# LSH attention with two gated MoE layers on one core: head 0's hash bits in a pair of score banks, a later identity load, and idle matmuls in the first gap

## The chip, the cores and the metric

One core of one Trainium2 chip runs the whole program in one launch. The metric is device time in microseconds (us), the median of several executions. A profiled execution has its own time beside it, and a span from its first to its last instruction.

## The reference, cut to what matters

```python
q_bits = (einsum('bhsd,dk->bhsk', q, proj) > 0)      # 6 bits for each of 768 positions, 16 heads of 64
k_bits = (einsum('bhsd,dk->bhsk', k, proj) > 0)
mask = bucket(q_bits)[..., :, None] == bucket(k_bits)[..., None, :]
scores = where(mask, scale * q @ k.T, -1e9)
attn = softmax(scores)                               # then attn @ v
x = attn_out as (1536, 512)
h = x @ w_in;  g = max(h, 0) + alpha * min(h, 0);  y = g @ w_out
h2 = y @ w_in2;  g2 = P(h2) / (Q(h2) + 1e-6);      out = g2 @ w_out2    # P cubic, Q = 1 + |b0||h2| + |b1|h2^2
```

All data are float32. The second half has d_model 512 and d_ff 2048.

## The kernel before, in words

**Work per head.** q and k come in transposed, 64 rows of 768 columns, held twice over 128 partitions. `k2` and `qh` are rounded copies of k and q, `kx` is what is left of k (and minus k on the lower rows), `ql` what is left of q. A row block of 128 queries makes a score tile 128x768 in two PSUM banks, in two steps: `first` (qh against kx, two matmuls of 384 columns, L559) and `second` (ql against k2, two matmuls, L564). The hash bits stand in rows 64 to 75 of `ql` and of `k2`, so `second` needs them: equal bits leave a score alone, unequal bits push it far away. VectorE then clamps the score (L574), ScalarE takes the exponential with the row sum (L580), TensorE turns the block by six transposes against the identity `idf` (L606, called `flip`), ScalarE or VectorE takes it out of PSUM into `pt` (`take`), and after six blocks twelve matmuls multiply with v (`pv`, L649).

**Hash bits.** `bits_mm` (L480) multiplies q and k with the projection: four matmuls of 384 columns, two for q and two for k, into four strips of 32 partitions of one PSUM bank (tag `b`). For head 0 four VectorE operations `bits_at` (L489), each 12 partitions by 384 columns, compare with a threshold and write the bits right into `ql` and `k2`. Later heads use one operation on all strips (L485) and small DMAs (L496). Blocks 0 to 2 of head 0 need only three of the four `bits_at`, since their queries lie in the first half of q.

**The start.** The engines begin with a memset of `rt`, nine matmuls of zeros on it (`warm`, L833, results never read), the constants from ScalarE's DMA queue, and then on SyncE's queue in this order: the identity, k and q of head 0, two weight pieces, q and k for later heads, v. The score tiles rotate through three pairs of banks (tag `s`), which scores and flips share, in the order in which the program text creates them.

**Order of the work.** Nothing is ordered by hand. The code creates tasks with their buffers; a planner (`Plan.order`) gives each task a start time from assumed durations, and the instructions of all engines are emitted by these times. At each step it takes, among the tasks that can begin about first, the one with the highest rank plus bias:

```python
t = max((t for t in ready if t.at[1] <= low), key=lambda t: t.rank + t.bias)
```

The rank is the length of the chain behind the task. The bias, and factors that make the planner prefer one engine to another for a task that may run on several, stand in the table `FAVOUR` by kind of task. A dependency of data is `after`, one of order alone `follow`. Once emitted, each engine runs its instructions in that order. Outside the attention the same planner orders the weight conversions (VectorE and ScalarE split each weight into a high and a low part), the first layer's and the second layer's matmuls (L679, L695, L698: 512 columns each), and the activations.

Of the kernel before, what the change touches and what calls it, by code (L numbers as in the profile page):

```python
# [64 lines left out]
FAVOUR = {
    "a_abs": (62.5, {}), "a_abs2": (202.2, {}), "a_exp": (-128.3, {"act": 0.17}), "a_g": (215.5, {}),
    "a_log": (1470.9, {"act": 0.52}), "a_mul": (-173.3, {"dve": 0.41, "pool": 0.47}), "a_n1": (584.8, {"dvp": 0.91}),
    "a_n2": (0, {"dvp": 0.84}), "a_p0": (-441.7, {"act": 3.65}), "a_p1": (240.4, {"act": 4.27}),
    "a_prep": (-94.8, {}), "a_quad": (-13, {"dvp": 0.98}), "a_sq": (89.8, {"act": 2.63}),
    "a_sum": (284.5, {"dve": 8.45, "pool": 0.09}), "awayb": (10.5, {}), "back": (-63.1, {"act": 0.05, "dvp": 0.04}),  # L70
    "backb": (672.3, {"act": 0.11, "dvp": 17.38}), "banks": (604.6, {"none": 1.11}), "bits": (205.6, {"pe": 2.45}),
    "bits0": (392.1, {"pe": 1.69}), "bits_at0": (-21.4, {}), "bits_at1": (-74.2, {}), "bits_at2": (-64.8, {}),
    "bits_at3": (-18.9, {}), "bits_ev": (-82.2, {"dvp": 0.3}), "bits_evb": (-222.6, {"dvp": 2.87}),
    "bits_mv": (310.2, {"dma": 2.11}), "bits_mvb": (5.8, {"dma": 0.57}), "bitsb": (-952.5, {"pe": 0.94}),
    "c_abs": (-16, {"act": 0.63}), "c_bits": (1.7, {"dve": 5.95}),
    "c_hi": (103.9, {"act": 0.14, "dve": 2.31, "pool": 23.21}), "c_lo": (1216.6, {"dve": 0.24}),
    "c_load": (18.4, {"dma": 0.12, "none": 3.41}), "c_prep": (-597.3, {"dve": 0.7}), "c_tail": (0, {"act": 0.38}),
    "clamp": (-286.8, {"dvp": 2.08}), "clampb": (35.5, {"dvp": 8.19}), "e_abs": (206.6, {"act": 2.31}),
    "e_bits": (-1934.6, {"dve": 0.36}), "e_lo": (-449.7, {"dve": 1.15}), "e_load": (147.1, {"dma": 0.27}),
    "e_out": (492.7, {}), "e_tail": (-99.1, {"act": 0.42}), "expo": (0, {"act": 0.67}),  # L80
    "expob": (-266, {"act": 1.51}), "eye": (239.2, {"dma": 2.17}), "f_abs": (-100.4, {"act": 1.32}),
    "f_bits": (-6, {}), "f_lo": (101.1, {"dve": 1.31}), "f_load": (819.2, {}), "f_out": (18.8, {}),
    "f_tail": (-511.9, {"act": 1.09}), "first": (239.8, {}), "flip": (4, {}), "flipb": (194, {"pe": 0.78}),
    "g_both": (-4.2, {}), "g_both0": (-3, {"dvp": 0.77}), "g_both1": (0, {"dvp": 0.39}),
    "g_hi": (-560.6, {"act": 0.68, "dvp": 47.43}), "g_hi0": (259, {"act": 5.33, "dvp": 1.56}),
    "g_hi1": (-238, {"act": 0.02, "dvp": 0.87}), "g_hi2": (-458.1, {"act": 0.14, "dvp": 0.3}), "g_lo": (142, {}),
    "g_lo0": (-144.9, {"dvp": 0.28}), "g_lo1": (2, {"dvp": 1.07}), "g_lo2": (251.9, {"dvp": 0.85}),
    "g_neg": (587.5, {"act": 1.54}), "g_neg0": (159.4, {"act": 6.17}), "g_neg1": (-0.9, {"act": 7.94}),
    "guard": (-19.6, {}), "guardb": (-1503.1, {"dve": 1.6}), "k2": (-9.1, {"act": 4.28, "dve": 50.0, "pool": 2.03}),
    "k20": (-339.4, {"act": 0.24, "dve": 32.94, "pool": 50.0}),  # L90
    "k2b": (28.3, {"act": 0.26, "dve": 1.26, "pool": 0.08}), "kx": (18.4, {"dve": 2.0}), "kx0": (0.7, {}),
    "kxb": (-433.4, {"dve": 8.17}), "load": (14.8, {"dma": 8.2}), "load0": (1.8, {}), "load2": (-302.2, {}),
    "load2b": (-81.7, {}), "loadb": (-131.6, {"dma": 2.11}), "o_add1": (-4732, {"dvp": 2.93}), "o_add2": (5.8, {}),
    "o_ev": (717.8, {"act": 1.21, "dvp": 0.02}), "o_ev0": (-19.1, {"act": 2.26, "dvp": 18.44}),
    "o_ev2": (632.5, {"act": 18.15, "dvp": 0.03}), "over": (-468.4, {"dvp": 0.04}), "overb": (271.3, {"dvp": 0.48}),
    "pv": (-688, {"pe": 1.11}), "pvb": (40.1, {}), "qh": (-33.7, {"act": 0.02, "dve": 0.44, "pool": 9.08}),
    "qh0": (-225.7, {"act": 1.4, "dve": 50.0, "pool": 0.11}),
    "qhb": (395.9, {"act": 0.03, "dve": 10.86, "pool": 0.02}), "ql": (366.3, {"dve": 7.18, "pool": 0.32}),
    "ql0": (106, {"dve": 8.57, "pool": 0.12}), "qlb": (12.8, {"dve": 10.81, "pool": 7.82}),
    "recip": (-2.7, {"dve": 2.0}), "recipb": (-158.2, {"dve": 0.51}), "reload": (-163.2, {"dma": 0.45}),  # L100
    "s1": (-17, {"pe": 0.73}), "s10": (-1021.8, {}), "s11": (-871.8, {"pe": 1.31}), "s12": (12.5, {}),
    "s2": (-121.5, {"pe": 5.53}), "s20": (0, {"pe": 2.84}), "s21": (-42.4, {"pe": 0.75}),
    "scores": (-47.9, {"pe": 2.11}), "scores0": (-8.7, {}), "scoresb": (53.1, {}), "second": (-269.4, {}),
    "swap": (-61.6, {}), "take": (7.1, {"act": 0.02, "dvp": 50.0}), "takeb": (0, {"act": 0.02, "dvp": 0.11}),
# [936 lines left out]
```

## Time and profile before

| what | value |
|---|---|
| median of 3 runs | 757.69 us (756.81 to 758.21) |
| profiled execution, its own time | 757.42 us |
| its span | 755.6 us |
| PE (TensorE) busy in the span | 744.4 us, 99% |
| mean granted TensorE clock | 0.997 of full |

The first two rows are device times, of unprofiled runs and of the execution that left the profile. The span leaves out what lies before the first and behind the last instruction. PE is TensorE's matmuls, PEld its weight loads, DVE VectorE, ACT ScalarE, POOL GpSimd, SP SyncE; SPq marks DMA issues on SP's queue.

### The profile page before, as it was taken

The page shows a single profiled execution, that of the slowest core. Times are in us where ns is not written, and L with a number is a line of the kernel's source. Part 1 is how long each engine was busy: PE and PEld are TensorE (multiplying, and loading weights), DVE is VectorE, ACT ScalarE, POOL GpSimd, SP SyncE. Part 2 cuts the span into 40 slices and gives each one's busy share as a digit, 9 for nine tenths or more (in the row PEclk, how much of TensorE's full clock was granted, in tenths as well). Part 3 has the DMA queues.
Part 4 walks back from the last instruction along what each step waited for, and adds up shares of the span by engine and source line. Part 5 has one row for each costly group of instructions (what it writes and reads, how often), then busy time and mean ns, then how long its engine had stood idle before and what let it go on. Part 6 is the DMA issues. An engine that isn't in the chain of part 4 may idle for free.

```text
span 755.6 us, 10816 instructions
## 1 busy us (share of the span) xinstructions
PE 744.4 (99%) x3729; PEld 587.2 (78%) x3729; DVE 664.4 (88%) x1187; ACT 513.3 (68%) x881; POOL 146.2 (19%) x130
## 2 busy tenths in 40 slices
PE   7999999999999999999999999999999999999998
PEld 4677667676777888888888888888888888888886
DVE  6998999999989999998999899999898877778882
ACT  5889989978874654544454356887887686766660
POOL 4322211010000000000000000125533344433430
PEclk9999999999999999999999999999999999999999
DMA  6854666556332123256433652520202200200012
GB/s 231 238 172 132 184 181 162 175 189 190 121 109 67 72 96 112 100 179 194 139 108 117 208 173 93 195 112 1 111 1 112 111 1 1 111 1 1 14 57 97
DMA packets 36199, 88.21 MB, mean 117 GB/s; under 512 B 8800, under 2 KB 11952, under 8 KB 34608
## 3 DMA queue, kind: packets, MB, share of 16 engines
q1 hardware_dynamic: 35856, 87.35, 35.7%
q8 instruction: 29, 0.48, 0.2%
q14 instruction: 26, 0.21, 0.1%
q10 hardware_dynamic: 288, 0.17, 0.1%
HBM read 70.62 MB, written 15.78 MB: 114 GB/s over the span
## 4 chain that ended last, share of the span: by engine, by line
PE 93%; DMA 4%; DVE 2%; issue 1%; SPq 0%; POOL 0%; ACT 0%; DVEq 0%; ACTq 0%; POOLq 0%
PE h L679 35%; PE o L698 17%; PE o L695 16%; PE pv L649 8%; PE t L606 7%; PE s L559 4%; PE s L564 4%; DMA rq<-qT 2%; PE h L695 1%; DMA rq<-qN 1%; PE pb L480 1%; DVE x L574 1%; DVE acc L655 0%; DMA k<-bt 0%; DVE kx L466 0%
## 5 line engine op out<-in xcount | busy, mean ns | idle before, releaser
L679 PE MATMUL h<-xh,wih 128*128 128x512 f32 x384 | 150.2, 391 | 0.0
L679 PE MATMUL h<-xl,wih 128*128 128x512 f32 x384 | 149.8, 390 | 0.0
L679 PE MATMUL h<-xh,wil 128*128 128x512 f32 x384 | 149.4, 389 | 0.0
L574 DVE TENSOR_SCALAR_CACHE_REDUCE x<-s 128x768 f32<-128x768 f32 x96 | 90.8, 953 | 7.3 <-PE s L564 6.2
L580 ACT ACTIVATE x<-x,st 128x768 f32<-128x768 f32 x96 | 89.3, 931 | 8.3 <-DVE x L574 4.9
L606 PEld LDWEIGHTS t<-idf,x 128*128 128x128 f32 x576 | 65.8, 141 | 24.3 <-issue 8.5
L429 ACT ACTIVATE pt<-t 128x768 f32<-128x768 f32 x91 | 73.0, 806 | 16.8 <-PE t L606 16.5
L679 PEld LDWEIGHTS h<-xl,wih 128*128 128x128 f32 x384 | 72.1, 188 | 15.5
L679 PEld LDWEIGHTS h<-xh,wil 128*128 128x128 f32 x384 | 72.1, 188 | 15.2
L679 PEld LDWEIGHTS h<-xh,wih 128*128 128x128 f32 x384 | 72.1, 188 | 14.9
L606 PE MATMUL t<-idf,x 128*128 128x128 f32 x576 | 80.7, 277 | 2.8 <-ACT x L580 1.9
L744 POOL TENSOR_TENSOR x<-x,ap 128x512 f32<-128x512 f32 x48 | 62.5, 1303 | 100.6 <-ACT x L732 63.9
L698 PE MATMUL o<-woh,gl 128*128 128x512 f32 x192 | 74.9, 390 | 0.0
L698 PE MATMUL o<-woh,gh 128*128 128x512 f32 x192 | 74.8, 390 | 0.0
L698 PE MATMUL o<-wol,gh 128*128 128x512 f32 x192 | 74.8, 390 | 0.0
L649 PE MATMUL pv<-pt,vr 128*64 128x384 f32 x384 | 68.8, 494 | 0.0
L695 PE MATMUL o<-gh,wol 128*128 128x512 f32 x176 | 68.6, 390 | 0.0
L695 PE MATMUL o<-gh,woh 128*128 128x512 f32 x176 | 68.6, 390 | 0.0
L695 PE MATMUL o<-gl,woh 128*128 128x512 f32 x176 | 68.5, 389 | 0.0
L438 DVE TENSOR_TENSOR gl<-h,gh 128x512 fp32r<-128x512 f32 x96 | 64.8, 684 | 2.3 <-ACT gh L429 1.6
L429 ACT ACTIVATE gh<-h 128x512 fp32r<-128x512 f32 x72 | 43.0, 601 | 28.6 <-DVE h L718 16.9
L329 ACT ACTIVATE raw<-raw 128x512 uint32<-128x512 uint32 x64 | 43.0, 672 | 25.9 <-DMA raw<-w_out 12.9
(97 smaller groups left out, 1449.3 us busy)
## 6 DMA issues: line engine op xcount, KB each, us to landing
raw<-w_in SPq DMA_DIRECT2D x32, 512.0 KB
raw<-w_out SPq DMA_DIRECT2D x32, 512.0 KB
rk<-kT SPq DMA_DIRECT2D x16, 384.0 KB
rq<-qT SPq DMA_DIRECT2D x16, 384.0 KB
sp<-mag SPq DMA_DIRECT2D x24, 256.0 KB
sp<-w SPq DMA_DIRECT2D x16, 256.0 KB
vr<-vN SPq DMA_DIRECT2D x8, 384.0 KB
rs<-rd SPq DMA_DIRECT2D x32, 96.0 KB
```

The costliest lines, as they stand in the source:

```text
L329: s_.activation(self.low, self.low, AF.Copy, scale=2.0 ** -9 * (1 - 2.0 ** -22))
L429: s_.activation(out, in_, AF.Copy, scale=scale)
L438: eng[e].tensor_tensor(out, a, b, op=ALU.subtract)
L559: te.matmul(sp[:, j, :HALF], K["qh"][:, q], K["kx"][:, j * HALF:(j + 1) * HALF], start=True, stop=False)
L574: v_.tensor_scalar(x.rearrange("p (j c) -> p j c", j=2), T["s"][:, :, :HALF], SCALE, FAR, op0=ALU.mult, op1=ALU.min, accum_out=T["st"])
L580: s_.activation(T["x"], T["x"], AF.Exp, bias=T["st"], scale=-1.0, accum_out=tr["ss"][:, half, tt:tt + 1])
L606: te.transpose(o[:, c], T["x"][:, c], idf)
L649: te.matmul(T["pv"][64 * half:64 * half + 64, :HALF], tv["vr"][:, m, kt, :], E[half][0]["pt"][:, kt, :], start=(kt == 0), stop=(kt == NT - 1))
L679: te.matmul(hp, wt[:, kc, f], xt[:, kc], start=(n == 0), stop=(n == 3 * KC - 1))
L695: te.matmul(op, lt[:, m, d], rt, start=(n == 0), stop=(n == 3 * FT - 1))
L698: te.matmul(op, lt[:, d], rt[:, m], start=(n == 0), stop=(n == 3 * FT - 1))
L744: eng[e].tensor_tensor(P[a], P[a], P[b], op=op)
```

## The change

- **Bits of head 0.** Four matmuls as before, but into a pair of banks of tag `s`: q in partitions 0 to 31, k in 64 to 95, the two halves of the columns in the two banks. Two `bits_at` of 12 partitions by 768 columns write them down, one for `ql`, one for `k2`. All blocks of head 0 need both. The pair takes the first slot of the rotation, so the blocks' slots move on by one (`WIDE` by one more).
- **Identity.** Its load follows the load of head 0's q on SP's queue instead of standing ahead of it.
- **Matmuls without use.** Eight more matmuls of zeros (`again`), after `second` of block 2 of head 0, into the bank that `warm` used.
- **Text order.** In head 0 three blocks, not two, are created before the first flip, which changes the order in which scores and flips take slots.
- **Planner.** The assumed wire time of head 0's q goes from 1.0 to 1.6, and nearly all entries of `FAVOUR` (bias and engine factors) are new. So the emitted order of the whole program can differ.

```diff
+AGAIN = 8
 FAVOUR = {
...
-    "eye": (239.2, {"dma": 2.17}),
+    "eye": (-66.1, {"dma": 2.17}),
...
-    "qh0": (-225.7, {"act": 1.4, "dve": 50.0, "pool": 0.11}),
+    "qh0": (656.5, {"act": 0.19, "dve": 2.91, "pool": 0.02}),
...
-    "take": (7.1, {"act": 0.02, "dvp": 50.0}), "takeb": (0, {"act": 0.02, "dvp": 0.11}),
+    "take": (339, {"act": 0.02, "dvp": 5.94}), "takeb": (103.5, {"act": 0.03, "dvp": 0.73}),
...
-WIDE = (3, 2 * NT * HW)
+WIDE = (3, 2 * NT * HW + 1)
...
+        def bits0_mm(e):
+
+            T["b"] = bank_pair("pb0")
+            for j in range(2):
+                for n, r in enumerate(("rq", "rk")):
+                    te.matmul(T["b"][64 * n:64 * n + 32, j, :HALF], Z[n], T[r][:, j * HALF:(j + 1) * HALF],
+                              start=True, stop=True)
+
...
         def bits_at(n):
-            to, j, r = T["ql" if n < 2 else "k2"], n % 2, slice(32 * n, 32 * n + 2 * NB)
-            v_.tensor_scalar(to[64:64 + 2 * NB, j * HALF:(j + 1) * HALF], P["b"][r, :HALF],
-                             cst[r, 0:1], cst[r, 1:2], op0=ALU.is_ge, op1=ALU.mult)
+            r = slice(64 * n, 64 * n + 2 * NB)
+            v_.tensor_scalar(T["k2" if n else "ql"][64:64 + 2 * NB].rearrange("p (j c) -> p j c", j=2),
+                             T["b"][r, :, :HALF], cst[r, 0:1], cst[r, 1:2], op0=ALU.is_ge, op1=ALU.mult)
...
-            plan.send("load" + z, load(n, src), 0.4, 1.0, (), [r])
+            plan.send("load" + z, load(n, src), 0.4, 1.6 if h == 0 and n == "rq" else 1.0, (), [r])
...
-        if h < 2 or h % 2 == 0:
+        if h == 0:
+            b = plan.buf("s")
+            plan.add("bits0", bits0_mm, {"pe": 0.98}, [*R, BZ], [b], cols=1536)
+        elif h == 1 or h % 2 == 0:
...
-            B["at"] = [Buf() for n in range(4)]
-            for n in range(4):
-                plan.add(f"bits_at{n}", lambda e, n=n: bits_at(n), {"dvp": 0.7}, [b, *([B["kx"]] * (n > 1))], [B["at"][n]])
+            B["at"] = [Buf() for n in range(2)]
+            for n in range(2):
+                plan.add(f"bits_at{n}", lambda e, n=n: bits_at(n), {"dvp": 0.88}, [b, *([B["kx"]] * n)], [B["at"][n]])
...
-            at = [BK["at"][half], *BK["at"][2:]]
+            at = BK["at"]
...
-                plan.add("second", second, {"pe": 0.35}, [BK["ql"], BK["k2"], *at], [B["s"]], cols=614)
+                u = plan.add("second", second, {"pe": 0.35}, [BK["ql"], BK["k2"], *at], [B["s"]], cols=614)
+                if t == 2:
+                    w = plan.add("again", again, {"pe": 0.2267 * AGAIN}, [BR], [BPV], cols=512 * AGAIN)
+                    w.after([u])
...
+    PV = {}
+
     def warm(e, count=WARMUP):
 
-        o = tl(ps, "pv", [128, 512], F32, "warm")
+        if not PV:
+            PV["o"] = tl(ps, "pv", [128, 512], F32, "warm")
         for n in range(count):
-            te.matmul(o, rt[:, :128], rt, start=True, stop=True)
+            te.matmul(PV["o"], rt[:, :128], rt, start=True, stop=True)
+
+    def again(e):
+        warm(e, AGAIN)
...
-    plan.send("eye", eye_load, 0.42, 0.25, (), [BE])
+    EYE = plan.send("eye", eye_load, 0.42, 0.25, (), [BE])
...
+    EYE.follow(plan.tags["raw_qk"][1].writers[0])
...
-            wait(2)
+            wait(3 if h == 0 and t < NT - 1 else 2)
```

## Rows read from the trace of the kernel before

**Rows 1.** The page's busy table: engine, busy us, share of the span, instructions.

```profile
PE 744.4 (99%) x3729; PEld 587.2 (78%) x3729; DVE 664.4 (88%) x1187; ACT 513.3 (68%) x881; POOL 146.2 (19%) x130
```

**Rows 2.** Busy time by stretch: length, engines, granted clock, DMA share, GB/s.

```profile
1.40:6.10 4.70, 4.22 (x11) 2.85 (x12) 1.27 (x5) 2.09 (x3) 1.17 (x4) 1.00 0.87 258
6.10:12.90 6.80, 3.92 (x21) 2.35 (x21) 5.38 (x11) 3.02 (x6) 2.66 (x2) 1.00 0.98 373
12.90:17.30 4.40, 4.28 (x24) 2.88 (x24) 3.71 (x7) 3.56 (x7) 1.62 (x3) 0.61 0.32 124
17.30:31.30 14.00, 12.69 (x87) 8.24 (x83) 12.96 (x27) 12.13 (x22) 5.82 (x4) 1.00 0.68 195
31.30:200.00 168.70, 167.28 (x1113) 119.95 (x1110) 157.81 (x315) 147.60 (x258) 28.76 (x31) 1.00 0.59 174
200.00:750.00 550.00, 550.00 (x2479) 449.55 (x2478) 482.02 (x826) 344.66 (x589) 105.39 (x82) 1.00 0.27 93
750.00:755.60 5.60, 2.04 (x9) 1.34 (x8) 0.80 (x3) 0.00 (x0) 0.00 (x0) 0.91 0.27 94
```

**Rows 3.** The same view in stretches of 1 us around the lower clock.

```profile
13.00:14.00 1.00, 1.00 (x9) 1.00 (x9) 0.96 (x4) 1.00 (x3) 0.00 (x0) 0.93 0.98 384
15.00:16.00 1.00, 1.00 (x6) 0.67 (x4) 0.80 (x2) 0.33 (x1) 0.70 (x1) 0.50 0.06 22
17.00:18.00 1.00, 1.00 (x11) 0.52 (x4) 0.89 (x2) 1.00 (x4) 0.90 (x1) 0.86 0.00 0
```

**Rows 4.** The chain of waits, first 40 us: start, length, what.

```profile
8.89 7.26 DMA rq<-qT
16.19 1.42 PE pb L480 x8
...
22.18 0.43 PE s L564
...
23.11 7.35 DMA rq<-qN
...
30.50 0.85 PE pb L480 x8
```

**Rows 5.** Timeline of PE: start, length, instruction [idle before <- releaser].

```profile
1.45 4.21 PE L833 MATMUL warm<-rt 128*128 128x512 f32 x9 [1.45 <-DVE rt L858]
6.09 0.85 PE L480 MATMUL pb<-rq,zq 128*32 128x384 f32 x2 [0.43 <-DMA rq<-qT]
...
6.70 0.68 PE L480 MATMUL pb<-rq,zq 128*32 128x384 f32 x2
6.83 0.61 PE L480 MATMUL pb<-rk,zk 128*32 128x384 f32 x2
7.37 1.31 PE L559 MATMUL s<-kx,qh 128*128 128x384 f32 x6
9.69 1.28 PE L564 MATMUL s<-k,ql 128*128 128x384 f32 x6 [1.00 <-DVE k L489]
12.85 0.88 PE L606 MATMUL t<-idf,x 128*128 128x128 f32 x6 [1.88 <-ACT x L580]
```

**Rows 6.** Timeline of SP's queue.

```profile
0.73 0.38 SPq L844 DMA_DIRECT2D idf<-eye  x1
1.17 0.42 SPq L462 DMA_DIRECT2D rk<-kT  x1
```

**Rows 7.** Timeline of DVE and ACT.

```profile
7.48 0.69 DVE L489 TENSOR_SCALAR k<-pb,every 12x384 fp32r<-12x384 f32 x1 [1.27 <-PE pb L480]
...
9.57 0.67 DVE L489 TENSOR_SCALAR ql<-pb,every 12x384 fp32r<-12x384 f32 x1
...
10.30 0.43 DVE L338 TENSOR_SCALAR mag<-mag 128x512 f32<-128x512 f32 x1
...
10.76 0.96 DVE L574 TENSOR_SCALAR_CACHE_REDUCE x<-s 128x768 f32<-128x768 f32 x1
...
14.54 0.79 ACT L429 ACTIVATE pt<-t 128x768 f32<-128x768 f32 x1
```

More of the change, by code (lines that the diff above doesn't have):

```diff
@@ L71 @@
[L71 to L92, printed above, removed]
@@ L108 @@
[L108 to L112 removed]
+    "a_abs": (-88.3, {}), "a_abs2": (324.8, {}), "a_exp": (-201.2, {"act": 0.17}), "a_g": (-11.7, {}),
@@ new lines @@
+    "a_log": (17.3, {"act": 0.52}), "a_mul": (-448.2, {"dve": 1.24, "pool": 0.62}), "a_n1": (36, {"dvp": 0.91}),
+    "a_n2": (-41.5, {"dvp": 0.84}), "a_p0": (-236.2, {"act": 3.65}), "a_p1": (377.6, {"act": 4.27}),
+    "a_quad": (14.4, {"dvp": 0.98}), "a_sq": (11.1, {"act": 2.63}), "a_sum": (538.1, {"dve": 21.94, "pool": 0.07}),
+    "again": (227.4, {}), "away": (-138.6, {}), "awayb": (-8.9, {}), "back": (0, {"act": 0.05, "dvp": 0.04}),
+    "backb": (35.4, {"act": 0.11, "dvp": 17.38}), "banks": (-122.1, {"none": 1.11}), "bits": (155.7, {"pe": 2.45}),
@@ new lines @@
+    "bits0": (-354.9, {"pe": 1.69}), "bits_at0": (-496.3, {}), "bits_at1": (-811.2, {}),
+    "bits_ev": (-107.6, {"dvp": 0.3}), "bits_evb": (773.6, {"dvp": 2.87}), "bits_mv": (0, {"dma": 2.11}),
+    "bits_mvb": (-334.3, {"dma": 0.57}), "bitsb": (-905.6, {"pe": 0.94}), "c_abs": (0, {"act": 0.63}),
+    "c_bits": (-34.6, {"dve": 5.95}), "c_hi": (3.7, {"act": 0.16, "dve": 0.93, "pool": 20.78}),
+    "c_lo": (521.7, {"dve": 0.24}), "c_load": (18.8, {"dma": 0.12, "none": 3.41}), "c_prep": (-463.8, {"dve": 0.7}),
@@ new lines @@
+    "c_tail": (-41.9, {"act": 0.38}), "clamp": (-81.4, {"dvp": 2.08}), "clampb": (-7.4, {"dvp": 8.19}),
+    "e_abs": (-132.7, {"act": 2.31}), "e_bits": (-3077, {"dve": 0.36}), "e_lo": (-153.9, {"dve": 1.15}),
+    "e_load": (-541.4, {"dma": 0.27}), "e_out": (476, {}), "e_tail": (-523.3, {"act": 0.42}),
+    "expo": (41.7, {"act": 0.67}), "expob": (26.7, {"act": 1.51}), "eye": (-66.1, {"dma": 2.17}),
+    "f_abs": (-279.1, {"act": 1.32}), "f_bits": (-23.9, {}), "f_lo": (1247.2, {"dve": 1.31}), "f_load": (535.9, {}),
@@ new lines @@
+    "f_out": (25.1, {}), "f_tail": (-1291.2, {"act": 1.09}), "first": (79, {}), "flip": (-181.6, {}),
+    "flipb": (387.4, {"pe": 0.78}), "g_both": (55.8, {}), "g_both0": (73.1, {"dvp": 0.77}),
+    "g_both1": (-394, {"dvp": 0.39}), "g_hi": (-929.9, {"act": 0.1, "dvp": 18.51}),
+    "g_hi0": (182.2, {"act": 8.91, "dvp": 0.03}), "g_hi1": (-172.7, {"act": 0.02, "dvp": 0.46}),
+    "g_hi2": (-568.9, {"act": 0.17, "dvp": 1.07}), "g_lo": (-385.1, {}), "g_lo0": (-7.9, {"dvp": 0.28}),
+    "g_lo1": (1.6, {"dvp": 1.07}), "g_lo2": (160.8, {"dvp": 0.85}), "g_neg": (-21.4, {"act": 1.54}),
@@ new lines @@
+    "ql0": (-135.5, {"dve": 0.13, "pool": 0.03}), "qlb": (0, {"dve": 50.0, "pool": 49.26}),
+    "recip": (-182.1, {"dve": 2.0}), "recipb": (-620.4, {"dve": 0.51}), "reload": (486.4, {"dma": 0.45}),
+    "s1": (-133.5, {"pe": 0.73}), "s10": (185.5, {}), "s11": (0, {"pe": 1.31}), "s12": (3.2, {}),
+    "s2": (20.2, {"pe": 5.53}), "s20": (7.2, {"pe": 2.84}), "s21": (13.9, {"pe": 0.75}),
+    "scores": (41.4, {"pe": 2.11}), "scores0": (7.4, {}), "scoresb": (269.4, {}), "second": (-808.9, {}),
+    "swap": (177.6, {}), "take": (339, {"act": 0.02, "dvp": 5.94}), "takeb": (103.5, {"act": 0.03, "dvp": 0.73}),
@@ L161, in send @@
         t.wire, t.begin, t.ack, t.block = wire, begin, ack, block
+        return t
     @staticmethod
@@ L858, in lsh_attention_moe_moe @@
     plan.add("zero", lambda e: v_.memset(rt.bitcast(F32), 0.0), {"dve": 1.0}, writes=[BR])
-    plan.add("warm", warm, {"pe": 0.2267 * WARMUP}, [BR], [plan.buf("pv")], cols=512 * WARMUP)
+    BPV = plan.buf("pv")
+    plan.add("warm", warm, {"pe": 0.2267 * WARMUP}, [BR], [BPV], cols=512 * WARMUP)
     plan.add("c_load", consts_load, {"none": 3.1}, writes=[BZ])
     plan.add("c_prep", consts_prep, {"dve": 0.3}, [BZ], [BZ])
-    plan.send("eye", eye_load, 0.42, 0.25, (), [BE])
+    EYE = plan.send("eye", eye_load, 0.42, 0.25, (), [BE])
     plan.add("a_prep", last_prep, {"dve": 0.1}, [BZ], [BL])
```

42 lines of the change are left out of this document (18 added, 24 removed).

## The prediction

> **What bounds the kernel now.** First the busy table [rows 1]: TensorE is busy 744.4 of 755.6 us, idle 11.2. Then the windows [rows 2], to see where those 11.2 lie. Take the length of each stretch less PE's busy time: 1.40 before the first row, 0.48 to 6.1 us, 2.88 to 12.9, 0.12 to 17.3, 1.31 to 31.3, 1.42 from there to 200, nothing from 200 to 750, 3.56 in the last stretch (last evictions and stores). So 95% of the span is a full PE queue, and no edit at the front changes it except by bringing it forward. What can be won at the front is idle PE time between 1.4 and 31.3 us, 4.79 us, and time at the lower clock.
>
> For that, the clock column: 0.61 in the stretch 12.9 to 17.3 [rows 2]. The 1 us windows show the edges [rows 3]: 0.93, then 0.50, then 0.86, so from about 13.86 to 17.28 the lower level of 1.2 GHz is granted, 3.4 us. PE had been idle 1.88 us just before, from 10.97 to 12.85, and 1.00 us ahead of 9.69 [rows 5]. PE was busy in nearly all of the slow stretch, so about 3.3 x 0.5 = 1.65 us of it were lost.
>
> Next, what released the work at the front: the PE timeline [rows 5] and the chain of waits [rows 4]. The bits wait for head 0's q (6.09), `second` for VectorE's bits (9.69), the first flip for the exponential (12.85); later the chain is head 1's q, issued at 8.89 and landed at 16.15, its bits, and through small DMAs its `second` at 22.18; then the bits of a later pair, whose q lands at 30.46. Behind that PE waits almost never.
>
> **The change, part by part.** Times are on the profiled execution's axis.
>
> *Identity later.* Its issue takes SP from 0.73 until 1.17 [rows 6]; without it everything behind goes 0.44 us earlier. It also carried 64 KB, 0.25 us at 258 GB/s [rows 2], so head 0's q lands 0 (if the queue's rate alone sets it) to 0.69 us earlier; I take 0.44, the issue. It is used up to the point where `warm` holds PE: nine matmuls from 1.45 end at 5.66 [rows 5], against a start of the bits at 6.09. So the bits start near 5.65, 0.44 earlier. The identity itself is next late: one 64 KB transfer behind q, needed by the first flip at 12.85. Those 6 us are its cover; without them each 0.1 us of delay would reach the flip.
>
> *Bits in a pair of banks.* Before, the four matmuls sit in four different strips and run side by side: two sets of records, 0.61 us apart at the lower clock (6.09 and 6.70), done at 7.44 [rows 5]; at full clock all eight take 0.85 [rows 4]. Now q's two halves use the same strip, and k's two also, so the second half follows the first: four sets instead of two. At the lower clock that is 4 x 0.61 + 0.13 = 2.6 us, at full clock twice 0.85 less one drain, about 1.5. The level rose during the old bits (first record 0.85, last 0.61), near 7.0. From 5.65 to 7.0 some 2.2 sets pass, the other 1.8 take 0.3 each and a drain of 0.2: done at 7.75, against 7.44. Bounds: 7.15 (full clock throughout) and 8.25 (low throughout).
>
> *Two evictions instead of four.* They go at 0.695 us each (7.48 to 9.57 for three steps [rows 7]), but `second` waited only for three: 2.21 us from 7.48 to 9.69. The 12x768 form isn't in the trace. Below, the clamp of 128x768 follows its like by 0.88 and lasts 0.96 [rows 7]; above, two old ones, 1.39. I take 1.0, nearest to the clamp, which reads as many PSUM columns. So two take 2.0, and `second` starts near 7.8 + 2.0 + 0.15 = 9.95 instead of 9.69 (9.1 to 11.3). The edit removes an operation off the path and none on it.
>
> *Slots.* Block 2's `first` now needs the bank pair that the bits hold, so it can't run in the gap ahead of `second`; one pair, a third of the 1.05 us by which three are streamed (1.31 with the drain [rows 5]), moves behind the evictions. The three `second` and this `first` then end near 9.95 + 1.4 = 11.35.
>
> *First clamp.* It waited for a weight operation of 0.43 us at 10.30 and began at 10.76 [rows 7]. Now its score is ready near 10.6. From clamp to flip it was 2.09 us, so the exponential allows the flip at 12.7 (12.3 to 13.4).
>
> *The idle matmuls.* Eight at the full level are half of the old 0.47 us (4.21 / 9 [rows 5]), 1.9 in all: PE is taken until 13.2, so the first flip is 0.35 later than before. What hides it: the first `take` ran at 14.54 behind three exponentials [rows 7], while its flip ended at 13.73; without that cover the 0.35 counts in full. I count 0.3 lost up to here, bounds -0.5 and +1.5. In return the idle stretch that went before the fall of the clock is filled, and the 1.65 us come back (0 if the clock falls anyway).
>
> The trace keeps the full level through 31.3 to 200 us [rows 2], where flips are mixed with other matmuls. The Trainium skill, "TensorE: Matmul & The Clock Gate", Part 4, says that transposes don't count as activity for the clock the way matmuls do; by it the flips that follow the idle matmuls would do nothing for the level, it could fall again behind them, and the sum would be near -0.1. The mixture in the trace doesn't show flips alone, so it neither bears this out nor refutes it.
>
> *Up to 31.3 us.* Can PE use those 1.65? Between 12.85 and 22.18 before, 9.3 us, it had 1.65 of slow clock and about 0.5 of idle: 7.2 us of real work, which now could be done by 13.2 + 7.2 = 20.4. But head 1's `second` has its own chain: q landed at 16.15, 6.03 us before 22.18 [rows 4]. With q 0.44 earlier (same transfers ahead of it) and the bits at full clock (0.85, not 1.42) it comes at about 21.2. PE fills the difference with block 3's score, which the new text order allows before the first flip, and with `first` of head 1. Of the idle 0.12 + 1.31 I let 0.4 come back.
>
> *The reordered rest.* 31.3 to 200 lost 1.42 us, with VectorE busy 94% and ScalarE 87% of it [rows 2]. A new order can win these 1.42 or add waits; I take 0.
>
> Sum: +0.3 - 1.65 - 0.4 = -1.75. Against the execution's own 757.42 that is 755.67; it lies 0.27 under the median, so on the median's scale 757.69 - 1.75 = 755.9.
>
> **Rivals.**
> - *Transfers set it* (no change). Head 1's q stays at about 16.15, since the loads for later heads and the weights stand ahead of it, and all that PE does sooner is paid back waiting for it. For: the chain is a DMA from 8.89 to 16.15 [rows 4]. Against: the queue starts earlier. Only the shorter bits count, 0.57, and small change: 756.5 to 757.7.
> - *The idle matmuls block at the lower clock* (slower). Place: the gap between `first` and `second`, which grows from 1.0 to about 1.6 us because block 2's pair has left it and the evictions end later. If the level falls there, near 10.4, the four pairs behind take 2.8 and the eight matmuls 3.75, the first flip comes at 16.5, 3.65 later, less the 1.65 that fall away: 759.7. It decides once the granted clock of 10.5 to 13.5 reads 0.5. Against: before, a gap of 1.0 with 1.31 of matmuls in front was followed by 1.00 until 13.86. Beside it the Trainium skill, the same page, Part 1, says that the moment of the switch isn't tied to the kernel's start; no run here shows that, and this rival would then hold in some executions only.
> - *The new order adds waits* in 31.3 to 200. For: two engines near full [rows 2]. Each added wait like those there costs 0.3 to 1; four to six of them more than eat the gain: 758.5 to 760.
> - *More comes back*: the 1.42 us as well, and most of the 1.43 idle: -2.8 to -4.2, 753.5 to 754.9.
>
> **Chances.** A difference under 0.2% (1.5 us) can't be told from none here. Forecast (754.8 to 757.0) 0.42, of which 0.34 lie below 756.2; transfers 0.24; block at the lower clock 0.07; new waits 0.13; more comes back 0.14. Faster: 0.34 + 0.14 = 0.48; slower: 0.07 + 0.13 = 0.20; same: 0.24 + 0.08 = 0.32. The range, 753.3 to 759.3, takes in half of the new waits' reach and nearly all of the last rival; it leaves out the block at the lower clock, half of the new waits and little else, about 0.15. The forecast's own range is 754.8 to 757.0.
>
> **What would show it.** In the profile of the changed kernel: head 0's bits start near 5.65 and end near 7.75 in four sets; each L489 lasts about 1.0; `second` near 9.95; eight matmuls behind it at 0.22 to 0.24 us; a granted clock of 1.00 from 13 to 18; head 1's `second` near 21.2; idle PE of about 1 us from 13 to 31.3. The prediction is wrong if the clock reads 0.5 anywhere from 8 to 17, if head 1's q still lands at 16, or if PE's idle time between 31.3 and 200 is more than 2.5 us.

## The result and the profile after

The changed kernel takes 762.11 us (median of 4 runs, 761.17 to 763.0) beside 757.25 us for the kernel before (4 runs, 756.65 to 758.21): ratio 1.0065, with a 95% interval of 1.0052 to 1.0077, so 4.9 us slower, where 1.75 us faster was forecast and 759.3 was the end of the range. The profiled execution took 761.97 us, with a span of 760.2.

The busy table, against [rows 1]:

```profile
PE 747.3 (98%) x3737; PEld 589.6 (78%) x3737; DVE 659.1 (87%) x1184; ACT 520.4 (68%) x890; POOL 138.4 (18%) x122
```

PE is busy 2.9 us longer, 2.02 of it the eight idle matmuls and 0.9 the bits of head 0 (2.26 us from 5.58 to 7.84, before 1.35 from 6.09 to 7.44), and idle 12.9 us instead of 11.2: +2.9 and +1.7 are the 4.6 us by which the span grew. The windows, in the columns of [rows 2], tell where the idle time lies:

```profile
1.40:6.10 4.70, 4.65 (x11) 2.99 (x13) 1.38 (x5) 2.83 (x4) 1.28 (x5) 1.00 0.84 300
6.10:12.90 6.80, 5.31 (x26) 3.50 (x23) 3.84 (x5) 2.58 (x4) 1.70 (x1) 1.00 1.02 402
12.90:17.30 4.40, 4.26 (x32) 3.18 (x30) 4.28 (x11) 4.35 (x10) 0.84 (x1) 1.00 0.09 36
17.30:31.30 14.00, 10.80 (x69) 8.06 (x66) 10.72 (x19) 9.50 (x17) 5.26 (x3) 0.88 0.56 168
31.30:200.00 168.70, 166.34 (x1103) 119.03 (x1102) 154.25 (x310) 149.31 (x263) 30.84 (x31) 1.00 0.59 172
200.00:750.00 550.00, 549.34 (x2480) 447.70 (x2479) 482.00 (x831) 351.58 (x596) 97.65 (x76) 1.00 0.27 94
```

Up to 17.3 us the change does what it says: idle time 0.05, 1.49 and 0.14 where it was 0.48, 2.88 and 0.12, and the clock reads 1.00 instead of 0.61. Then it goes the other way. From 17.3 to 31.3 PE idles 3.20 us (1.31 before) at a clock of 0.88, and from 31.3 to 200 it idles 2.36 (1.42 before), with 0.66 more from 200 to 750. Counted as useful work, PE is about 3.0 us behind the kernel before at 31.3 us: 0.1 more idle time, 2.02 of idle matmuls, 0.9 for the longer bits, and the lower clock for 3.4 us as before. So of the 4.6 us, 3.0 lie up to 31.3 and 1.6 behind it. PE's timeline at the front, against [rows 5]:

```profile
5.58 0.85 PE L490 MATMUL pb<-rq,zq 128*32 128x384 f32 x1
...
7.35 0.49 PE L490 MATMUL pb<-rq,zq 128*32 128x384 f32 x1
...
10.21 0.59 PE L572 MATMUL s<-kx,qh 128*128 128x384 f32 x2 [1.49 <-DVE k L499]
10.64 1.23 PE L577 MATMUL s<-k,ql 128*128 128x384 f32 x6
11.70 2.02 PE L852 MATMUL warm<-rt 128*128 128x512 f32 x8
13.56 0.51 PE L572 MATMUL s<-kx,qh 128*128 128x384 f32 x2
...
14.27 0.81 PE L622 MATMUL t<-idf,x 128*128 128x128 f32 x6
...
22.18 0.59 PE L577 MATMUL s<-k,ql 128*128 128x384 f32 x2 [1.14 <-DMA ql<-bt]
...
27.07 0.52 PE L482 MATMUL pb<-rq,zq 128*32 128x384 f32 x2 [1.60 <-DMA rq<-qN]
...
31.67 2.16 PE L665 MATMUL pv<-pt,vr 128*64 128x384 f32 x12
```

Head 0's `pv` begins at 31.67, against 28.06 before. The wait of 1.60 at 27.07 is new in kind: in the new order the bits of heads 4 and 5 stand ahead of head 0's `pv` in PE's queue, and the q that they need, issued at 22.16, hasn't landed. Before, the `pv` went first:

```profile
28.06 2.16 PE L649 MATMUL pv<-pt,vr 128*64 128x384 f32 x12
30.50 0.52 PE L480 MATMUL pb<-rq,zq 128*32 128x384 f32 x2 [0.29 <-DMA rq<-qN]
```

The clock falls right behind this wait and reads 0.50 from about 27.7 to 31.1, 3.4 us as before, only later. Three of the four runs of the changed kernel have a mean clock of 0.998, which is what one such fall costs, and one has 1.0. The 1 us windows, against [rows 3]:

```profile
27.00:28.00 1.00, 0.93 (x9) 0.18 (x9) 0.00 (x0) 0.28 (x2) 0.00 (x0) 0.83 0.75 248
28.00:29.00 1.00, 1.00 (x7) 1.00 (x4) 0.97 (x2) 0.00 (x0) 0.18 (x1) 0.50 0.11 28
...
31.00:32.00 1.00, 1.00 (x6) 0.62 (x7) 0.22 (x1) 1.00 (x2) 0.00 (x0) 0.96 1.01 406
```

VectorE's timeline, against [rows 7]: the two writes of the bits, in their new form.

```profile
7.89 1.07 DVE L499 TENSOR_SCALAR ql<-pb,every 12x768 fp32r<-12x768 f32 x1 [1.90 <-PE pb L490]
8.99 1.07 DVE L499 TENSOR_SCALAR k<-pb,every 12x768 fp32r<-12x768 f32 x1
```

Of the 3.02 us of idle time behind 31.3 us, 2.16 lie between 70 and 135. How such a wait comes about is seen in the timelines of 67 to 77 us of SP's queue, VectorE, ScalarE and PE, in this order:

```profile
67.66 1.53 SPq L506 DMA_DIRECT2D ql<-bt  x2
```

```profile
70.25 0.43 DVE L342 TENSOR_SCALAR mag<-mag 128x512 uint32<-128x512 uint32 x1
72.39 0.68 DVE L495 TENSOR_SCALAR bt<-pb,every 128x384 fp32r<-128x384 f32 x1 [1.71 <-DMA ql<-bt]
72.99 0.95 DVE L587 TENSOR_SCALAR_CACHE_REDUCE x<-s 128x768 f32<-128x768 f32 x1
```

```profile
74.04 0.94 ACT L593 ACTIVATE x<-x,st 128x768 f32<-128x768 f32 x1 [1.70 <-DVE x L587]
```

```profile
76.73 0.61 PE L572 MATMUL s<-kx,qh 128*128 128x384 f32 x2 [0.44 <-ACT pt L431]
```

Read it from above. The small DMAs that bring a head's bits from `bt` into `ql` are issued at 67.66. `bt` has a single buffer, so VectorE's next write into it waits for them and VectorE stands 1.71 us, until 72.39. (Such an instruction, which waits at the head of its engine's queue and holds up all that is queued behind it, is called a *stand* below.) Behind it in VectorE's queue is a clamp, the exponential waits for the clamp, a take stands behind the exponential, and PE, which had work queued until then, waits 0.44 for that take at 76.73. None of these instructions is new. They are queued in another order.

### The profile page after: what moved, and what is told of

Same layout as the page of the kernel before. It is cut to its first block, busy times and chain, and to the rows that moved or that the text cites. A ratio compares the mean times of both kernels' runs of the same rounds, so it can differ in the third digit from the quotient of the medians.

```text
span 760.2 us, 10830 instructions
## 1 busy us (share of the span) xinstructions
PE 747.3 (98%) x3737; PEld 589.6 (78%) x3737; DVE 659.1 (87%) x1184; ACT 520.4 (68%) x890; POOL 138.4 (18%) x122
## 4 chain that ended last, share of the span: by engine, by line
PE 81%; DVE 2%; DMA 1%; ACT 1%; issue 0%; DVEq 0%; SPq 0%
PE h L695 34%; PE o L714 17%; PE o L711 16%; PE pv L665 4%; PE t L622 4%; PE s L572 2%; PE s L577 2%; PE h L711 1%; DMA raw<-w_in 1%; DVE x L587 1%; ACT x L593 0%; DVE acc L671 0%; DVE kx L468 0%; ACT pt L431 0%; DVE pt L435 0%
## 5 line engine op out<-in xcount | busy, mean ns | idle before, releaser
L431 ACT ACTIVATE pt<-t 128x768 f32<-128x768 f32 x95 | 76.0, 805 | 15.2 <-PE t L622 14.9
L431 ACT ACTIVATE gh<-h 128x512 fp32r<-128x512 f32 x79 | 46.5, 601 | 47.8 <-DVE h L775 26.7
L327 ACT ACTIVATE mag<-raw 128x512 f32<-128x512 f32 x64 | 42.8, 669 | 47.8 <-DMA raw<-w_in 25.5
```

The lines of the kernel that those rows point to most:

```text
L327: s_.activation(self.m, self.top.bitcast(F32), AF.Abs)
L431: s_.activation(out, in_, AF.Copy, scale=scale)
```

## The experiments

All have a fixed order: in place of the planner's own, the list of instructions is given, taken from the one kernel or the other, and single entries are moved. Only e1 and e11 let the planner order. Line numbers in the profiles of the others are some 100 higher for that. In the lists, `bits` is the bits matmuls, `bits_ev` VectorE's write of bits into `bt`, `qh`, `ql` and `kx` the operations that make these tiles, `over` and `recip` what scales the result of `pv`, and names with `w_` or `e_` are operations on weight pieces; a name that ends in b belongs to heads 8 to 15, and the number counts the tasks of that name. Besides the order, the changed kernel's list puts 64 of its 2655 tasks on another engine than the old one, so "order" below means both. Each ratio is to runs of the kernel before on the same chip.

**The parts by themselves.** e1 is the changed kernel without the idle matmuls (they are not issued); e2 to e4 are the kernel before in its own order with one part each; e5 has all three parts in the old order.

```diff
 e1
     def again(e):
-        warm(e, AGAIN)
+        pass
 e2, SP's queue
-eye  k(0)  q(0)
+k(0)  q(0)  eye
 e3, PE's queue
-second(2)  flip(0)
+second(2)  again  flip(0)
 e4, PE and VectorE: one pair of banks
-bits_at0  bits_at1  bits_at2  bits_at3
+bits_at0  bits_at1
```

> The changed kernel with its own order, but the eight idle matmuls behind block 2 are not issued. Theory (the loss comes from the new order: TensorE is brought to transfers and evictions that are not there yet, and head 1's second step stands at 22.18 us whatever TensorE does before): the first flip comes near 13 instead of 14.27, the clock falls between 14 and 17 us, and the time stays within 0.8 us of the changed kernel, 761.3 to 763. Rival (the idle matmuls themselves block TensorE and their time carries to the end): 1.5 to 2 us less than the changed kernel, about 760.

> The kernel before with its order of all instructions held, but the identity's load issued behind head 0's q. Theory: head 0's bits start near 5.65 instead of 6.09 and 0 to 0.4 us of it reach the end: 756.8 to 757.3 against 757.25. Rival (an earlier start only reaches the same transfer of head 1's q and the clock's fall): no difference under 0.1 us; a rise over 0.5 us would say that the place of the identity costs.

> The kernel before with its order held, and eight idle matmuls put behind the second step of block 2, nothing else. Theory: they fit in the idle stretch from 10.97 to 12.85, the granted clock stays at 1.00 from 13 to 18 us, and as head 1's chain bounds what can be used, 0.3 to 1.3 us less than before, 756.0 to 757.0. Rival (idle matmuls delay the first flip and cost): 0.5 to 1.5 us more than before.

> The kernel before with its order held, but with head 0's bits in a pair of score banks, two evictions of 768 columns, and block 2's first step behind them as in the changed kernel; identity first, no idle matmuls. Theory: bits end 1.2 us later than before at the lower clock, the second step starts near 11, and 0.3 to 1.2 us of it reach the end: 757.6 to 758.5. Rival (this part alone is the loss, since all later work stands behind it): 2.5 us or more over the kernel before.

> All three parts of the change (pair of banks with two evictions, identity behind q, idle matmuls), but every instruction in the order of the kernel before; only what the parts themselves move is moved. Theory (the new order is the loss): 756.9 to 758.5, within 1.5 us of the kernel before. Rival (the parts together make a loss that none makes alone, by a first flip that comes later): 760 or more.

| kernel | us | ratio (interval) |
|---|---|---|
| e1 changed, idle matmuls left out | 760.89 | 1.0062 (1.0040 to 1.0084) |
| e2 identity later, old order | 757.18 | 1.0007 (0.9994 to 1.0019) |
| e3 idle matmuls, old order | 757.77 | 1.0010 (0.9997 to 1.0023) |
| e4 pair of banks, old order | 757.67 | 1.0010 (0.9998 to 1.0023) |
| e5 all three, old order | 758.35 | 1.0013 (1.0000 to 1.0026) |

No part alone costs or wins anything that can be told from none, and all three together cost about 1 us (0 to 2.0). So some 4 of the 4.9 us come with the new order. e2, e4 and e5 came out within their forecasts; e3 missed its gain.

e1 lies between its two forecasts. Its median is 0.2 us under the changed kernel's by the ratios, give or take 1.9, so the medians alone don't clear the idle matmuls. Its trace says more: without them the first flip comes at 12.52 instead of 14.27, but head 1's `second` comes at 21.85 instead of 22.18, and the bits of heads 4 and 5 wait for their q until 27.25 (27.07 with them). So nearly all that the idle matmuls take would be idle time otherwise in the new order. The fall of the clock between 14 and 17 us that was forecast for e1 didn't come; its profile reads 1.00 there.

e3 shows what the idle matmuls do in the old order. Its clock stayed at 1.00 and head 0's `pv` began at 26.21, 1.85 us earlier than in the profile before. Part of this is the single execution: e15, a control below with the front of the kernel before, kept the full clock in its profile without idle matmuls and had this `pv` at 27.32. All of the 1.85 was gone in the end (the table of `pv` starts below). The windows of 31 to 60 and 150 to 200 us, first of the kernel before, then of e3:

```profile
31.30:60.00 28.70, 28.68 (x197) 20.92 (x194) 26.50 (x54) 24.64 (x44) 7.29 (x8) 1.00 0.60 191
150.00:200.00 50.00, 48.63 (x319) 34.29 (x316) 47.26 (x95) 41.37 (x73) 5.11 (x6) 1.00 0.57 176
```

```profile
31.30:60.00 28.70, 27.42 (x184) 19.60 (x183) 25.30 (x53) 24.29 (x44) 7.19 (x7) 1.00 0.60 180
150.00:200.00 50.00, 47.37 (x306) 32.86 (x303) 45.72 (x89) 39.51 (x69) 4.66 (x6) 1.00 0.55 169
```

PE idles 0.02 and 1.37 us there in the kernel before, and 1.28 and 2.63 in e3.

**Where in the order.** All parts are in; one order is cut at a `pv` and the other goes on from there.

```diff
 e6
-changed order throughout
+changed order up to head 0's pv, old order behind it
 e7
+old order up to head 0's pv, changed order behind it
 e9
+old order up to head 4's pv, changed order behind it
 e10
+changed order up to head 8's pv, old order behind it
```

> The changed kernel's instructions in its own order up to head 0's first product with v (some 31 us), everything behind it in the order of the kernel before. If the front makes the loss (by TensorE's useful work up to 31.3 us it is 3.0 us behind): 759 to 760.5. If the rest makes it, within 1 us of the kernel before.

> All three parts, in the order of the kernel before up to head 0's first product with v, everything behind it in the changed kernel's order. By the idle time of TensorE behind 31.3 us (3.02 us in the changed kernel, 1.42 before) 1 to 2.5 us over the kernel before, 758 to 759.5. If the front is the whole loss: within 1 us of the kernel before; if the rest is: 760.5 or more.

> All three visible parts; the instructions stand in the order of the kernel before up to head 4's first pv (near 80 us), and in the changed kernel's order from there on. Theory 'the cost lies in the new order behind head 4' (taken from the run with the seam at head 0, whose first three heads ran level and which lost 3.9 us behind them): 760 to 762, idle PE of 1.5 or more between 100 and 250 us. Rival 'the cost comes from the start, or from the first 80 us, of the new order': 758 to 759, as with all parts in the old order.

> The reverse: the changed kernel's order up to head 8's first pv (near 145 us), then the order of the kernel before. Theory 'the cost lies in the new order, ahead of 145 us as well as behind it': about 761 to 762, since the waits between 60 and 140 us stay; of the idle PE time behind 145 us, 0.86 in the changed kernel, at most that much can go. Rival 'it lies in the last heads of the attention': 758 to 759. A seam can add waits of its own of 1 to 3 us right behind 145, which the windows would show.

| kernel | us | ratio (interval) | idle PE 70 to 135 us |
|---|---|---|---|
| e6 | 763.56 | 1.0080 (1.0063 to 1.0096) | 0.00 |
| e7 | 761.10 | 1.0051 (1.0029 to 1.0073) | 3.67 |
| e9 | 759.21 | 1.0031 (1.0019 to 1.0043) | 1.68 |
| e10 | 763.62 | 1.0093 (1.0073 to 1.0114) | 1.84 |

The waits between 70 and 135 us go with the changed order there and vanish with the old one. e7, with the old front, still loses 2.9 us more than e5, which has the old order throughout (1.0013), so the changed order behind head 0 costs by itself, the seam where one order goes over into the other included. As a division of the loss the four runs are of little use: e6 and e10, which have the old order behind their seam, come out no faster than the changed order throughout (1.0065), since a seam adds waits of its own (e6 idles 3.44 us from 31 to 70). e6, e7 and e10 came out above the range held likeliest, and e9 between its two forecasts.

**The order's table.** e11 is the changed kernel with the old `FAVOUR`, ordered by the planner.

```diff
-FAVOUR = { ... of the changed kernel ... }
+FAVOUR = { ... of the kernel before ... }
```

> The changed kernel with the table FAVOUR of the kernel before; the planner makes an order of its own out of the two. Theory 'the new table is what costs': 758 to 759.5. Rival 'the old table is fitted to the old tasks, any order that isn't the old one as emitted loses': 760 to 765, with idle PE time of 3 or more between 31 and 250 us.

783.46 us, ratio 1.0354 (1.0333 to 1.0375). Its windows, and those of the changed kernel, in this order:

```profile
31.30:250.00 218.70, 209.57 (x1332) 148.27 (x1334) 196.64 (x381) 173.15 (x301) 29.66 (x31) 0.99 0.53 150
250.00:750.00 500.00, 492.30 (x2153) 403.40 (x2150) 435.48 (x733) 311.89 (x529) 109.72 (x85) 1.00 0.27 91
```

```profile
31.30:250.00 218.70, 215.68 (x1383) 154.27 (x1382) 197.94 (x394) 182.80 (x319) 32.92 (x34) 1.00 0.52 155
250.00:750.00 500.00, 500.00 (x2200) 412.46 (x2199) 438.30 (x748) 318.09 (x539) 95.57 (x73) 1.00 0.27 93
```

This lies far over both forecasts. So the new table isn't a bad one as such; it is far better for the new tasks than the old. A table belongs to its tasks: by the ratios, the same work is 22 us slower here than in the changed kernel's order, where only the planner's order and its choice of engines differ.

**The cause in 70 to 135 us.** The changed order, with the instructions later that stood for late data: three in e12, only VectorE's two in e16.

```diff
 e12 and e16, VectorE's queue
-bits_ev(3)  clamp(27)  clamp(28)
+clamp(27)  clamp(28)  bits_ev(3)
-bits_evb(0)  clamp(39)  clamp(40)
+clamp(39)  clamp(40)  bits_evb(0)
 e12, ScalarE's queue
-e_tail(1)  expob(3)  takeb(1)  takeb(2)  qhb(2)  takeb(3)
+expob(3)  takeb(1)  takeb(2)  qhb(2)  takeb(3)  e_tail(1)
```

> The changed kernel's own order with three instructions put later: two writes of hash bits on VectorE, which stood 1.71 and 1.13 us for the DMAs that still read their only buffer, each behind the two clamps that followed, and one ScalarE operation on a weight piece, which stood 0.79 us for the piece to land, behind the next four takes and exponentials. Theory 'VectorE's and ScalarE's queues stand behind an instruction whose data is late, and PE's waits between 70 and 135 follow from that': PE's idle time between 70 and 135 falls from about 2.2 us to 1 or less, and the time by about 1, to 761. Rival 'the engines are that late anyway and the wait only moves': idle time as before, 762.

> The changed kernel's own order with only the two writes of hash bits on VectorE put behind two clamps each, ScalarE's operation on the weight piece left where it was. With all three later the time fell from 762.1 to 758.7, PE's idle time from 70 to 135 from 2.16 to 0.02. If VectorE's two stands carry most of it: 759.3, idle 0.8 near 130. If ScalarE's alone carried it: 761.5.

e12: 758.67 us, ratio 1.0029 (1.0015 to 1.0043), so 2.7 us of the 4.9 (1.3 to 4.1) come back by three moves, more than the 1 us forecast. Of the runs with a mean clock of 1.0, e12's have a median of 758.2 (6 runs) and the changed kernel's only one took 761.17, which speaks against the clock as the cause. e16: 759.32, ratio 1.0025 (1.0012 to 1.0037). The windows of 70 to 100 and 100 to 135 us, first of the changed kernel, then of e12:

```profile
70.00:100.00 30.00, 29.02 (x192) 20.68 (x192) 25.61 (x54) 26.35 (x46) 7.51 (x7) 1.00 0.57 148
100.00:135.00 35.00, 33.82 (x220) 22.80 (x216) 31.88 (x64) 29.27 (x53) 4.22 (x5) 1.00 0.57 172
```

```profile
70.00:100.00 30.00, 30.00 (x203) 21.48 (x203) 27.83 (x58) 27.44 (x49) 7.50 (x7) 1.00 0.60 162
100.00:135.00 35.00, 34.98 (x232) 24.49 (x229) 32.53 (x63) 30.44 (x54) 4.37 (x6) 1.00 0.58 170
```

2.16 us of idle PE become 0.02, and the span shrinks by 2.2. The gain is made where the moves are: head 3's first `pv` begins at 72.23 in e12 and 71.87 in the changed kernel, head 8's at 136.99 and 139.41. In e12's VectorE timeline the clamps run on time and the write of the bits (L604 here) finds its buffer free, without a wait:

```profile
70.98 0.96 DVE L696 TENSOR_SCALAR_CACHE_REDUCE x<-s 128x768 f32<-128x768 f32 x1
...
72.34 0.96 DVE L696 TENSOR_SCALAR_CACHE_REDUCE x<-s 128x768 f32<-128x768 f32 x1 [0.39 <-PE s L686]
...
73.22 0.68 DVE L604 TENSOR_SCALAR bt<-pb,every 128x384 fp32r<-128x384 f32 x1
```

e16 keeps ScalarE's stand for the weight piece and 1.14 us of idle time in the same stretch, so VectorE's two carry about half of it in the profile; the rest is a wait of 0.81 at 127.5 and one of 0.32 at 121.5, both for a take in ScalarE's queue. The medians of e12 and e16 don't tell the two apart.

**The front.** e8 moves the bits of heads 4 and 5 behind head 0's `pv` (the two loads that reuse their buffers go with them); e18 adds e12's three moves and three more, for the instructions that stood in e8.

```diff
 e8, PE's queue
-bits(2)  scores(2)  flip(6)  scores(3)  pv(0)
+scores(2)  flip(6)  scores(3)  pv(0)  bits(2)
 e18 besides, VectorE's queue
-qh(1)  w_lo(0)  clamp(8)  clamp(9)
+w_lo(0)  clamp(8)  clamp(9)  qh(1)
-qh(2)  recip(1)  over(0)  over(1)  clamp(13)
+recip(1)  over(0)  over(1)  clamp(13)  qh(2)
 e18, ScalarE's queue
-w_tail(2)  expo(12)  w_abs(2)  take(10)
+expo(12)  w_abs(2)  take(10)  w_tail(2)
```

> The changed kernel with its own order, but the bits matmuls of the pair of heads whose q lands at 27 us (TensorE waited 1.60 us there, and the clock fell behind it) are issued behind head 0's first product with v, and the two loads that reuse their buffers behind them. Theory (TensorE is brought to a transfer that has not landed): 1 to 2.5 us less than the changed kernel, 759.6 to 761.1. Rival (the wait only moves to the next late thing): within 0.6 us of the changed kernel, 761.5 to 762.7.

> The changed kernel's own order with the three instructions later (758.67 in that run), head 0's second bits later as in the run that moved them behind head 0's first pv, and three more that stood for a load then: VectorE's copies of q for heads 2 and 3 (1.89 and 1.64 us), each behind the next clamps, with the POOL operations that need them, and one ScalarE operation on a weight piece (1.17), behind the next exponential and take. Theory 'each of these stands is PE's wait a little later': idle PE time from 17.3 to 31.3 falls from 3.5 to about 2, from 31.3 to 60 it stays under 0.5 (2.49 in the run that moved the bits alone), the clock keeps the full level, and the time falls to about 757.2, level with the kernel before. Rival 'the wait only moves, as it did there': 759 to 761.

e8: 763.06 us, ratio 1.0071 (1.0057 to 1.0085). e18: 761.18, ratio 1.0053 (1.0041 to 1.0066). Neither brought the gain of its theory; by the ratios e8 is level with the changed kernel, as its rival had it, and e18 lies just above its rival's range. In e8 head 0's `pv` begins at 26.76 instead of 31.67, and the two stands on VectorE that e12 removes grow from 1.71 and 1.13 us to 2.43 and 1.91:

```profile
72.08 0.68 DVE L605 TENSOR_SCALAR bt<-pb,every 128x384 fp32r<-128x384 f32 x1 [2.43 <-DMA ql<-bt]
100.25 0.68 DVE L605 TENSOR_SCALAR bt<-pb,every 128x384 fp32r<-128x384 f32 x1 [1.91 <-DMA ql<-bt]
```

PE idles 4.21 us from 70 to 135 there, where it idled 2.16 in the changed kernel. So an earlier front only lengthens the wait at these two. e18, in which they are moved, has these windows:

```profile
17.30:31.30 14.00, 12.32 (x87) 8.38 (x86) 13.34 (x22) 11.07 (x20) 5.04 (x3) 1.00 0.50 154
31.30:60.00 28.70, 24.84 (x166) 18.03 (x165) 26.02 (x49) 22.64 (x40) 6.67 (x6) 1.00 0.67 184
```

The wait at 27 is gone, the clock is full and 1.68 us of idle time are left up to 31.3, but 3.86 follow up to 60, at 33.5, 41.8, 46.2 and 51.0. So at the front the wait does only move: there it matters what the moved instruction feeds, and which chain is late there these runs don't settle.

**The old order, with its own stands moved.** If an earlier start is given back at instructions that stand for data, then moving them should keep it. The stands of e3 and e5 were VectorE's write into `bt` at 41 us and two ScalarE copies of q at 154 and 182 (of heads 12 and 14; the expectations, also that of e17 for `kx`, misname them 10 and 11).

```diff
 e13 (all parts), e14 (idle matmuls alone), e15 (no part), VectorE's queue
-bits_ev(2)  clamp(14)  clamp(15)
+clamp(14)  clamp(15)  bits_ev(2)
-qlb(4)  clampb(18)
+clampb(18)  qlb(4)
 ScalarE's queue (and the same for qlb(6), qhb(6))
-qhb(4)  takeb(15)  expob(17)
+takeb(15)  expob(17)  qhb(4)
 e17: e14, and
-kxb(4)  ...  clampb(19)
+clampb(19)  kxb(4)      (and the same for kxb(6))
```

> All three visible parts in the order of the kernel before (758.36 in its run), with five instructions put later: VectorE's write of hash bits that stood 1.18 us at 41 for the DMAs still reading its buffer, behind the next two clamps; two ScalarE copies of q (heads 10 and 11) that stood 1.55 and 1.89 us for a q load to land, behind the next take and exponential; and the two VectorE operations that need these copies, behind the next clamp. Theory 'an earlier start is given back because an in-order queue stands behind data that isn't earlier': idle PE time from 31 to 60 falls from 0.94 to about 0, from 150 to 200 from 2.4 to about 1, and the time to about 756.5. Rival 'the wait only moves': 758 to 759.

> The kernel before with the eight idle matmuls alone (757.77 in its run), in the old order with the same five instructions later. Its head 0 reached pv 1.85 us earlier and gave that back in waits from 31 to 60 (1.28) and from 150 to 200 (2.63). Theory: both fall, by 2 us or more together, and the time to about 755.5, faster than the kernel before by 1 us. Rival: the wait only moves, 757.5 to 758.

> The kernel before with none of the parts, and the same five instructions later: the control. It had only 0.17 us of VectorE's wait at 41, 1.02 of ScalarE's at 154 and 1.37 us of idle PE from 150 to 200. Theory: 0.5 to 1 less, about 756.2. If it comes out as low as the run with the idle matmuls, an earlier start is worth nothing; if it is slower than before, the five moves do harm of their own.

> The kernel before with the eight idle matmuls alone, the five instructions later, and two more: VectorE's kx of heads 10 and 11 behind the next clamp. With five later (757.01 in its run) heads 1 to 9 ran 1.4 to 2.2 us earlier than before and half of that went back at PE's waits of 0.48 at 158 and 1.35 at 186, both for a clamp behind ql and kx in VectorE's queue. Theory: idle PE time from 150 to 200 falls from 2.29 to about 1.3 and the time to 756.2. Rival 'these waits move on to ScalarE, which is as late': 757.

| kernel | us | ratio (interval) |
|---|---|---|
| e13 all parts | 757.78 | 1.0006 (0.9996 to 1.0016) |
| e14 idle matmuls alone | 757.01 | 0.9998 (0.9984 to 1.0013) |
| e15 no part | 757.49 | 1.0005 (0.9992 to 1.0019) |
| e17 idle matmuls, more later | 759.46 | 1.0038 (1.0019 to 1.0056) |

Start of the first `pv` of a head in us, from the traces:

```
head    before    e3       e14      e15
0        28.06    26.21    26.36    27.32
1        41.88    39.92    39.83    40.79
2        57.08    56.45    55.00    55.97
9       149.10   148.47   146.96   147.98
11      176.43   176.27   174.60   175.68
15      234.76   235.87   233.09   234.59
```

The move at 41 us does what was expected: e14 idles 0.00 from 31 to 60, where e3 idled 1.28, and stays 2.1 us ahead of the kernel before up to head 9. From 150 to 200 it idles 2.29 us all the same (2.63 in e3), now mostly for clamps. The windows of 31 to 60 and 150 to 200 us, first of e14, then of the control e15:

```profile
31.30:60.00 28.70, 28.70 (x194) 20.93 (x193) 26.39 (x55) 25.55 (x46) 8.20 (x9) 1.00 0.61 194
150.00:200.00 50.00, 47.71 (x316) 34.38 (x314) 46.98 (x92) 42.13 (x73) 4.91 (x6) 1.00 0.58 172
```

```profile
31.30:60.00 28.70, 28.69 (x194) 20.88 (x193) 26.60 (x55) 25.55 (x46) 7.40 (x8) 1.00 0.57 190
150.00:200.00 50.00, 47.30 (x314) 34.08 (x312) 46.43 (x92) 40.81 (x72) 4.78 (x6) 1.00 0.58 172
```

e15 is the fairer comparison: it has the same five moves and kept the full clock in its profile too. Without any part it runs up to 1.1 us ahead of the kernel before, and from 150 to 200, where it idles 2.70, it gives most of that back. Beside it, e14 leads by 1.0 us from head 0 to head 9 and by 1.5 at head 15, so in these two traces the lead that the idle matmuls give isn't lost. The medians, 757.01 and 757.49, don't show it: both are level with the kernel before, e13, e14 and e15 all missed their theories' gains, and nothing measured here is faster than the kernel before. e17's edit was a slip: `kx` of heads 12 and 14 now stands behind the DMA that puts the bits into `k2`, which it reads. So it takes in those rows and waits for that DMA:

```profile
158.44 1.02 DVE L584 SCALAR_TENSOR_TENSOR kx<-k,low,rk 128x768 fp32r<-128x768 f32 x1 [0.84 <-DMA k<-bt]
```

It says nothing on the two theories, only once more what an instruction in the wrong place costs.

## Why the prediction was wrong, by its steps

- **Identity, bits, evictions: right.** Bits from 5.58 to 7.84 in four sets (5.65 and 7.75 forecast), evictions of 1.07 (1.0).
- **Slots: a step missed.** Block 2's `first` was costed behind the evictions, not in the path. In PE's queue it stands ahead of all three `second` and waits for the bank pair that the bits held until 10.06. So `second` came at 10.64, not 9.95, and with block 3's score ahead of it the first flip at 14.27, not 13.2.
- **Idle matmuls and clock: right in the mechanism, wrong in the sum.** Eight took 2.02 (1.9 forecast), 13 to 18 us ran at 1.00, and the level held through the flips behind them until 27.7. The 1.65 us were put down as won for good, but in the profile they were lost again at 27 us, where the new wait was followed by 3.4 us of the lower level. And 1.65 was too much for a median: the mean clock reads 1.0 in some executions of the kernel before and less in the others, whose medians lie 0.3 to 1.3 us apart in five sets of runs (756.34 and 757.35 in the first).
- **"Up to 31.3 us": the first step that failed.** The sum had PE 1.75 us ahead by here; by useful work it was 3.0 behind. The span was to shrink by 1.75 us and grew by 4.6; of this miss of 6.4 us, 4.8 lie here. PE was to fill its time with block 3's score and head 1's `first` and to idle about 1 us from 13 to 31.3; it idled 3.3. Head 1's `second` came at 22.18 to the digit as before, not at 21.2. Its q wasn't what was late, since PE shows no wait for it: the bits stood behind flips and a score in PE's queue until 16.69 and were done at 17.5 (17.6 before), so all that follows, the write into `bt` and the small DMAs, came when it had come before. The other wait, 1.60 us at 27.07, is for a load that the prediction named (the later pair's q, landed at 30.46 before) and for which it put down no wait. Before, PE reached it behind head 0's `pv`; the new order puts it ahead.
- **"The reordered rest ... I take 0": the second.** This term stood at nothing without a reason. The profile has 1.6 us more idle PE behind 31.3, and e12 took 2.7 us off the time by moving three of its instructions. The rival "the new order adds waits" named the mechanism with a chance of 0.13 and ended at 760; [rows 2] spoke for it more than it was given, with VectorE 94% and ScalarE 87% busy. The prediction's own sign for it, more than 2.5 us of idle time from 31.3 to 200, stayed just unmet at 2.36.

In sum: the loss of 4.9 us comes with the new order and its placement on engines, since with all three parts in the old order 1.0 (0 to 2.0) is left (e5 against the changed kernel). In e12, three moved stands between 70 and 135 us take off about 2.7 (1.3 to 4.1 by the two intervals). About 2.2 (1.1 to 3.3) are left against the kernel before, and by e12's trace they lie up to 31.3 us, since behind it PE idles less than in the kernel before (1.0 us up to 750, before 1.42). What sets this part stays open: e8 and e18 brought head 0's `pv` from 31.67 to 26.76 and 27.23 and lost it again. e5's 1.0 can't be taken off as a share of it, for there the front is early and the time is lost behind 31.3 (3.37 us of idle PE up to 200). That a wait of PE follows from a stand for late data in another engine's queue is shown for 70 to 135 us (e12, and e8 from the other side) and for e14's 41 us; at the front, moving the stands did not help (e18).
